# A planner that knows TensorE's array configuration and its drain, with step durations and ranks set anew

## The chip, the cores and the metric

The kernel runs on one core of a Trainium2 chip. The metric is the time of one execution on the device in microseconds, as the median of several runs; a profiled execution has its own time, given below. The core has five engines that run beside each other, each through its own list of instructions in order: TensorE (PE in the profile: matmuls and transposes), VectorE (DVE), ScalarE (ACT), GpSimd (POOL) and SyncE (SP, which issues most DMA transfers).

## What is computed

The reference, cut to what matters:

```python
# attention: q, k, v (4, 8, 576, 64), s (4, 8, 576)
scores = scale * np.matmul(q, k.transpose(0, 1, 3, 2))
cum = np.cumsum(np.maximum(s, 0.0), axis=-1)
bias = -(cum[:, :, :, None] - cum[:, :, None, :])
scores = np.where(causal, -1e9, scores + np.minimum(bias, 0.0))
x = softmax(scores) @ v                       # x: (4, 576, 512)
# gated value: a causal convolution over 5 positions gives the gate
gate = sigmoid(sum(conv_w[k] * xp[:, k:k + S, :] for k in range(5)))
x = (gate * (x @ w_val)) @ w_out
# experts: one of 8 per token, kept from the token before where a local gate says so
h = np.maximum(x[b, s] @ w1[e], 0.0)
out[b, s] = p[e] * (h @ w2[e])
```

## The kernel before, in words

The kernel has two parts. The first computes attention, the gated value, the product with `w_out` ("x2") and the routing of tokens to experts. The second (`ffn`) runs the eight experts in an order written by hand.

**Attention** goes by 16 pairs of heads (4 batches x 4 pairs). For a pair, q and k are turned on TensorE (`qk_main`, `qk_rest` for the last 64 rows), and split into a high and a low part (ScalarE, VectorE). `unit` makes the scores of a tile of 128 rows: for the tiles t < 4 both heads at once, each on 64 rows of the array (eight matmuls, line 653); for the last tile (t = 4) on the whole array (line 648). VectorE takes the minimum out of PSUM (680, 693), ScalarE the exponential (701), GpSimd scales (725), TensorE turns the result (737), ScalarE copies it out, and `pv` multiplies with v, one head in each half of the array's columns (789). Pairs 0, 1 and 4 (`LAY`) turn q and k by column halves too (533). Then GpSimd splits x (`hi`, `lo`, 803 and 807), VectorE makes the gate's five taps (814, 816) and ScalarE its tanh (821).

**value** (eight groups of twelve matmuls a batch, line 868) multiplies with `w_val`; VectorE multiplies with the gate (874). **x2_tile** (929) multiplies with `w_out`, in two halves of columns; **route** places tokens by VectorE scans and small transposes (1020, 1049). The weights `w_val` and `w_out` arrive as 64-bit numbers; `from_f64` turns them into 32-bit ones in five steps, on VectorE but for an absolute value that stands on ScalarE where `f64A` is 1 (272). `warm_up` adds steps of three small matmuls (415) that compute nothing; there are `nwarm` of them.

**The planner.** All these steps are not written out in order. Each is added to a `Plan` with its engine, an estimate of its duration, the steps it follows, the buffers (`slot`s) it holds and a rank (lower is sooner). `Plan.order` then simulates the engines: again and again it takes for each engine the first step by rank that could start at once, or else the one that can start earliest, and of these the earliest of all. The order found is the order in which the instructions are given to the engines; on the chip only that order is left of the plan, and each engine waits in it for its inputs. `SIZES` says how many buffers a name has: 4 "s" banks of PSUM for scores and pv, 2 "t" banks for the turned weights, 2 "m" banks for the turns of q and k, value, x2 and routing, 2 of "x", 5 of "xh", "xl" and "g". `RANKS` holds the numbers from which the ranks are made: for pair p the attention steps have about p, the taps p + `tap`, the split p + `split`, the value groups of batch b 4b + 4 + `val` + `dval` i, and so on. The plan doubles the duration of a TensorE step where TensorE was little used in the window before (`WINDOW`, `DUTY`).

Of the kernel before, what the change touches and what calls it, by code (L numbers as in the profile page):

```python
# [35 lines left out]
LAY = (0, 1, 4)  # L36
# [6 lines left out]
RANKS = dict(pv=-2.111, split=3.54, tap=31.589, load=2.389, front=1.118, norm=0.295, val=-0.561, dval=1.983, x2=19.035, dx2=-0.809, x2b=18.109, dx2b=2.149, x2h=16.913, send=47.523, split15=2.926, r2=11.61, xe=51.526, w=0.265, wo=1.268, nwarm=41, qP=2, merge=1, r0=10.835, r1=10.302, f64A=1, dwo=1.405)  # L43
WINDOW = 10.24 / 3
DUTY = 0.43
ISSUE = 0.6
NEXT = {"ACT": 0.06, "DVE": 0.13, "Pool": 0.1}
# [4 lines left out]
class Step:  # L52


    def __init__(self, eng, cost, f, after, on, rank, lat, rows):
        self.eng, self.cost, self.f, self.after, self.on, self.rank, self.lat = eng, cost, f, after, on, rank, lat
        self.fin, self.rows = None, rows
# [10 lines left out]
class Plan:  # L68
# [8 lines left out]
    def add(self, eng, cost, f, *after, on=(), rank=None, lat=0.17, rows=1.0):  # L77
        if eng == "PE" and lat < 1:
            lat += 0.06
        st = Step(eng, cost, f, after, on, self.rank if rank is None else rank, lat, rows)  # L80
        for sl in on:
            sl.left += 1
        self.steps.append(st)
        return st

    def order(self):
        n = len(self.steps)
        place = {st: i for i, st in enumerate(sorted(self.steps, key=lambda st: st.rank))}
        waits, users, at = {}, {st: [] for st in self.steps}, dict.fromkeys(self.steps, 0.0)
        ready = {st.eng: [] for st in self.steps}  # L90
# [4 lines left out]
        for st in self.steps:  # L95
            before, todo = set(), list(st.after)
            while todo:
                a = todo.pop()
# [10 lines left out]
        free = dict.fromkeys(ready, 0.0)  # L109
        held = {tag: [] for tag in self.sizes}  # L110
        order, use, moved = [], {}, 0.0
# [13 lines left out]
        while len(order) < n:  # L125
            best = None
            for eng, steps in ready.items():
                first = None
                for _, st in steps:
                    t = max(free[eng], at[st], opens(st))  # L130
                    if first is None or t < first[0]:
                        first = (t, st)
                        if t <= free[eng]:
                            break
                if first and (best is None or first[0] < best[0]):
                    best = first
            t, st = best
# [9 lines left out]
            if st.eng == "PE" and cost:  # L147

                if use.get(int(t / WINDOW) - 1, 0.0) < DUTY * WINDOW:
                    cost *= 2  # L150
                a, rest = t, cost
                while rest > 1e-9:
                    w = int(a / WINDOW + 1e-9)
                    d = min(rest, (w + 1) * WINDOW - a)
                    use[w] = use.get(w, 0.0) + d * st.cost / cost * st.rows
                    a, rest = a + d, rest - d
# [19 lines left out]
def build(tc, q, k, v, s, w_val, conv_w, w_out, w_gate, w_local, w1, w2, out, dbg=None):  # L176
    nc = tc.nc
    with ExitStack() as ctx:
# [23 lines left out]
        def c_pe(n):  # L202
            return n / 2350
# [75 lines left out]
        def constants():  # L279
# [33 lines left out]
            ready["ident"] = add("Pool", 1.1, lambda: make_identity(nc, ident), rank=-9)  # L313
            ready["zeros"] = add("Pool", 0.6, zeros, rank=-5)
            ready["mask"] = add("Pool", 1.6, triangles, rank=-4)
            ready["small"] = add("Pool", 1.5, small_ones, rank=0.5)
# [30 lines left out]
        def bias_rows():  # L347
# [51 lines left out]
            w = ready["gr_set"] = add("Pool", 2.6, gr_set, on=[sg])  # L399
            c = add("DVE", 1.1, scan, d, o, on=[ss, s1, sc])  # L400
            k, r = None, []
            for z in range(2):
                k = add("DVE", 0.68 if z else 0.4, lambda z=z: keys(z), c, w, k, on=[sc, sg])
                p = R["qP"] > z
                r.append(add(*(("Pool", 1.0) if p else ("ACT", 0.95)), lambda z=z, p=p: queries(z, p), k, on=[sg]))
# [114 lines left out]
        def qk_main(p, nm, loaded, sn, free):  # L520
# [27 lines left out]
            t = add("PE", 1.05 if p in LAY else 0.43, turn, loaded, ready["ident"], free, on=[sn, sm])  # L548
# [49 lines left out]
        def attention(p):  # L598
# [31 lines left out]
            def unit(u):  # L630
# [27 lines left out]
                for z in range(2 if t == 4 else 1):  # L658
                    m = add("PE", c_pe(4 * N), lambda z=z: prod(z), kq, r_, bd,
                            on=into + (banks[z:z + 1] if t == 4 else banks))  # L660
                    qk_read[p].append(m)
                    for i in (z,) if t == 4 else range(2):
                        ms[i] = m
# [161 lines left out]
            for half in range(2):  # L825
                sps = slot("s")
                m = add("PE", 2.4 if half else 0.72, lambda half=half: pv(half), evs[half], vl, rv[0],
                        on=[sps, sx, sv, rv[1]])
                pv_done[p][half] = m
                xo.append(add("ACT", c_act(320 if half else 256), lambda half=half: x_out(half), m, on=[sps, sx]))  # L830
# [18 lines left out]
        def value(b, ranks, after=None, sm_tag="m"):  # L849
# [5 lines left out]
            for i in range(8):  # L855
# [39 lines left out]
                m = add("PE", c_pe(12 * 288), prod, al, [x[0] for x in xd], [w_done[j] for j in range(4)],  # L895
# [10 lines left out]
        def x2_tile(b, t, ranks):  # L906
# [11 lines left out]
            for c0, c1, rank in ((256, WO, ranks[0]), (0, 256, ranks[1])):  # L918
# [35 lines left out]
                a = add("PE", c_pe(12 * (c1 - c0)), prod, y_steps[b, 0], y_steps[b, 1] if t > 1 else None,  # L954
# [169 lines left out]
        def route(b):  # L1124
# [5 lines left out]
            def step(eng, cost, f, *after, on=(), lat=0.17):  # L1130
                r.append(add(eng, cost, f, r[-1:], *after, on=on, lat=lat))
                return r[-1]
# [13 lines left out]
            step("DVE", 1.75, lambda: one[b].rank())  # L1146
# [521 lines left out]
```

## Time and profile before

| | us |
|---|---|
| median of 3 runs | 619.55 (618.77 to 622.70) |
| profiled execution | 616.59 |
| its span, first to last instruction | 614.8 |
| first matmul of the experts (line 1375) starts at | 363.53 |
| mean granted TensorE clock | 0.984 |

Busy times are of the hardware profiler. TensorE's matmuls are pipelined and overlap each other in the records, so their start times are what tells the pace. "Granted clock" 1.00 is 2.4 GHz, 0.50 is 1.2 GHz.

### The profile page before, as it was taken

How to read it: one execution, taken by the hardware profiler on the slowest of the kernel's cores; microseconds unless marked ns; L12 is line 12 of the kernel's file. 1: busy time of each engine (PE TensorE's matmuls, PEld its weight loads, DVE VectorE, ACT ScalarE, POOL GpSimd, SP SyncE). 2: the span in 40 equal slices, each digit the busy share in tenths (PEclk: the TensorE clock that was granted, in tenths of full speed). 3: DMA queues.
4: the chain of work that ended last, by engine and by line, in shares of the span. 5: the costliest groups of instructions: out<-in, count | busy, mean ns of one | idle time of the engine just before them, and what ended most of it. 6: DMA issues, size and time to landing. Idle time of an engine off the chain costs nothing. (4 is left out here: it accounts for less than half of the span.)

```text
span 614.8 us, 12466 instructions
## 1 busy us (share of the span) xinstructions
PE 577.8 (94%) x4346; PEld 503.3 (82%) x4346; DVE 410.5 (67%) x1029; ACT 339.4 (55%) x869; POOL 243.7 (40%) x377
## 2 busy tenths in 40 slices
PE   5899989999899988999989989999999999999994
PEld 4677678778777887777979987898998999999894
DVE  5589999968887668886699356455353636465550
ACT  2669868787478953677334325544243536355440
POOL 8367868553543433464550344030404004033101
PEclk8989999999999998999999999999999999999997
DMA  7734322322132310210133725273645537365710
GB/s 163 130 92 144 91 81 77 86 55 64 46 87 64 81 47 27 63 28 29 26 125 136 139 59 164 79 245 111 196 171 171 190 107 253 104 244 171 263 47 29
DMA packets 82838, 68.96 MB, mean 112 GB/s; under 512 B 60557, under 2 KB 66829, under 8 KB 82740
## 3 DMA queue, kind: packets, MB, share of 16 engines
q1 hardware_dynamic: 78788, 58.24, 33.2%
q0 software_dynamic: 3984, 9.88, 4.8%
q8 instruction: 36, 0.59, 0.4%
q14 instruction: 30, 0.25, 0.2%
HBM read 57.90 MB, written 10.79 MB: 112 GB/s over the span
## 5 line engine op out<-in xcount | busy, mean ns | idle before, releaser
L725 POOL TENSOR_SCALAR tt<-tt,st 128x512 f32<-128x512 f32 (+2 forms) x144 | 93.0, 661 | 103.0 <-DVE st L714 52.0
L1308 DVE TENSOR_TENSOR wl<-raw,wh 128x1024 fp32r<-128x1024 f32 x64 | 78.3, 1224 | 34.2 <-ACT wh L1305 33.8
L701 ACT ACTIVATE tt<-tt,st 128x384 f32<-128x384 f32 (+3 forms) x144 | 83.2, 583 | 12.4 <-DVE st L680 8.6
L1375 PE MATMUL h<-xth,wh 128*128 128x256 f32 (+5 forms) x256 | 73.7, 306 | 1.4 <-DVE xtl L1115 1.4
L1375 PE MATMUL h<-xth,wl 128*128 128x256 f32 (+5 forms) x256 | 72.9, 302 | 0.0
L680 DVE CUSTOM_DVE_ANT_0 tt<-s,mask 128x512 f32<-128x512 f32 (+3 forms) x128 | 57.9, 483 | 13.9 <-PE s L653 7.5
L1458 POOL DMA_INDIRECT out_dram<-out,id x21 | 28.6, 1362 | 96.7 <-ACT out L1456 83.3
L1305 ACT ACTIVATE wh<-raw 128x1024 fp32r<-128x1024 f32 x64 | 66.5, 1052 | 0.3 <-DMA raw<-in_moe_w_dram 0.3
L816 DVE SCALAR_TENSOR_TENSOR g<-x,cw,g 128x576 f32<-128x576 f32 x64 | 64.8, 1012 | 0.7
L737 PE MATMUL t<-ident,tt 128*128 128x128 f32 x384 | 61.9, 283 | 3.5 <-POOL tt L725 2.2
L1381 ACT ACTIVATE hh<-h 128x256 fp32r<-128x256 f32 (+5 forms) x64 | 27.1, 425 | 58.5 <-PE h L1375 52.1
L1382 DVE SCALAR_TENSOR_TENSOR hl<-h,hh 128x256 fp32r<-128x256 f32 (+5 forms) x64 | 29.8, 469 | 43.4 <-ACT hh L1381 43.4
L737 PEld LDWEIGHTS t<-ident,tt 128*128 128x128 f32 x384 | 43.3, 142 | 15.7 <-POOL tt L725 8.1
L1340 POOL DMA_INDIRECT xg<-x2d,id x20 | 20.9, 1046 | 87.2 <-DMA id<-ids 59.2
L929 PE MATMUL x<-wo_h,yl 128*128 128x266 f32 (+3 forms) x144 | 43.2, 300 | 7.8 <-DVE y L874 2.9
L653 PE MATMUL s<-QK 64*128 64x256 f32 (+2 forms) x384 | 48.9, 356 | 1.2 <-DVE st L693 1.2
L1375 PEld LDWEIGHTS h<-xth,wh 128*128 128x128 f32 x256 | 48.3, 189 | 1.9 <-DVE xtl L1115 1.6
L1375 PEld LDWEIGHTS h<-xth,wl 128*128 128x128 f32 x256 | 48.4, 189 | 0.2
L789 PE MATMUL pv<-PT,nv 128*64 128x320 f32 (+3 forms) x384 | 47.3, 386 | 0.0
L1375 PE MATMUL h<-xtl,wh 128*128 128x256 f32 (+5 forms) x256 | 46.3, 302 | 0.0
L929 PE MATMUL x<-wo_h,yh 128*128 128x266 f32 (+3 forms) x144 | 41.6, 289 | 0.0
L929 PE MATMUL x<-wo_l,yh 128*128 128x266 f32 (+3 forms) x144 | 41.6, 289 | 0.0
(269 smaller groups left out, 1499.4 us busy)
## 6 DMA issues: line engine op xcount, KB each, us to landing
raw<-in_moe_w_dram SPq DMA_DIRECT2D x64, 512.0 KB
nv<-in_v_dram SPq DMA_DIRECT2D x32, 128.0 KB
x2d<-x SPq DMA_DIRECT2D x32, 128.0 KB
nk<-in_k_dram SPq DMA_DIRECT2D x26, 128.0 KB
nq<-in_q_dram SPq DMA_DIRECT2D x26, 128.0 KB
wsc<-in_moe_w_val_dram SPq DMA_DIRECT2D x4, 512.0 KB
wsc<-in_moe_w_out_dram SPq DMA_DIRECT2D x4, 512.0 KB
nk<-in_k_dram SPq DMA_DIRECT2D x3, 256.0 KB
```

The lines of the kernel that those rows point to most:

```text
L653: nc.tensor.matmul(ps[hh][:, 0:N], lhsT=q[:, P * t:P * t + P], rhs=k[:, 0:N], start=n == 0, stop=n == 3)
L680: nc.vector.tensor_tensor_reduce(out=tl["tt"][:, 0:W], in0=ps[h][:, 0:W], in1=mask[:, 512 - W:512], scale=1.0, scalar=3.0e38, op0=ALU.add, ...
L701: nc.scalar.activation(tt[:, 0:W], tt[:, 0:W], AF.Exp, bias=st[:, 0, i:i + 1], scale=-1.0, accum_out=st[:, 1, i:i + 1])
L725: nc.gpsimd.tensor_scalar(tl["tt"][:, 0:W], tl["tt"][:, 0:W], st_["st"][:, 2, i:i + 1], 1.0, ALU.mult, ALU.mult)
L737: nc.tensor.transpose(ps[:, j], tl["tt"][:, P * j:P * j + P], ident)
L789: nc.tensor.matmul(tl["ps", half][64 * h:64 * h + 64, c:c + w], lhsT=vt[0:K, j, h] if j < 4 else vr[:, 2 * hp + h], rhs=(PT1 if half else ...
L816: nc.vector.scalar_tensor_tensor(tl["g"], x[:, t:t + S], cw[:, hp, t:t + 1], tl["g"], ALU.mult, ALU.add)
L929: nc.tensor.matmul(ps[0:m, 0:c1 - c0], lhsT=yy[:, kc] if both else yy[:, kc, P * t:P * t + m], rhs=wt_[:, kc, c0:c1], start=n == 0, stop=n ...
L1305: nc.scalar.activation(hi, raw, AF.Copy)
L1308: nc.vector.tensor_tensor(lo, raw, fv(hi), ALU.subtract)
L1375: nc.tensor.matmul(ps[:, 0:N], lhsT=w[:, P * f:P * f + P], rhs=xx[:, kc, c], start=n == 0, stop=n == 11)
L1382: nc.vector.scalar_tensor_tensor(hl[:, c], ps[:, 0:N], 0.0, fv(hh[:, c]), ALU.max, ALU.subtract)
```

## The change

The planner's model of TensorE is changed and all numbers that it works with are set anew. What each engine computes stays the same, but for three choices in `RANKS`: no warm-up steps (`nwarm` 41 to 0), one of the two query rows of the bias on ScalarE instead of GpSimd (`qP` 2 to 1), and the absolute value in the conversion of weights on VectorE instead of ScalarE (`f64A` 1 to 0).

A step gets a `mode`: "whole" (the default), "rows" (scores of t < 4) or "columns" (pv, and the turns of q and k of the pairs in `LAY`). In `order`, when the first TensorE step by rank has another mode than the last one, a step of the same mode that can start within 0.05 us and whose rank is at most `R_MODE` (2.332) higher is taken instead. A change of mode costs `SWITCH` (0.2 us) in the plan. The durations of matmul groups get a part for each matmul, and several durations of other engines are changed. The diff, cut to its core:

```diff
@@ -40,10 +40,12 @@
     return ap.bitcast(F32)
-RANKS = dict(pv=-2.111, split=3.54, tap=31.589, load=2.389, front=1.118, norm=0.295, val=-0.561, dval=1.983, x2=19.035, dx2=-0.809, x2b=18.109, dx2b=2.149, x2h=16.913, send=47.523, split15=2.926, r2=11.61, xe=51.526, w=0.265, wo=1.268, nwarm=41, qP=2, merge=1, r0=10.835, r1=10.302, f64A=1, dwo=1.405)
+RANKS = dict(pv=-14.891, split=3.794, tap=15.492, load=2.105, front=1.145, norm=0.197, val=-11.824, dval=0.089, x2=25.546, dx2=-5.125, x2b=11.419, dx2b=3.236, x2h=37.933, send=63.151, split15=1.095, r2=-13.208, xe=68.451, w=20.124, wo=-0.731, nwarm=0, qP=1, merge=1, r0=-2.243, r1=-0.613, f64A=0, dwo=1.274)
 WINDOW = 10.24 / 3
 DUTY = 0.43
 ISSUE = 0.6
+SWITCH = 0.2
+R_MODE = 2.332
 NEXT = {"ACT": 0.06, "DVE": 0.13, "Pool": 0.1}
 SIZES = dict(m=2, s=4, t=2, n=4, qk=2, G=2, gr=1, st=3, tt0=2, tt1=3, tt2=3, tt3=3, tt4=2, x=2, g=5, xh=5, xl=5, y=2,
              raw=4, x2=4, w=1, wf=1, nq=1, nk=1, nv=1, rq=1, rk=1, rv=1, lgs=4)
@@ -52,9 +54,9 @@
 class Step:
-    def __init__(self, eng, cost, f, after, on, rank, lat, rows):
+    def __init__(self, eng, cost, f, after, on, rank, lat, rows, mode):
         self.eng, self.cost, self.f, self.after, self.on, self.rank, self.lat = eng, cost, f, after, on, rank, lat
-        self.fin, self.rows = None, rows
+        self.fin, self.rows, self.mode = None, rows, mode
 class Slot:
@@ -74,10 +76,10 @@
     def slot(self, tag):
         return Slot(tag)
-    def add(self, eng, cost, f, *after, on=(), rank=None, lat=0.17, rows=1.0):
+    def add(self, eng, cost, f, *after, on=(), rank=None, lat=0.12, rows=1.0, mode="whole"):
         if eng == "PE" and lat < 1:
-            lat += 0.06
-        st = Step(eng, cost, f, after, on, self.rank if rank is None else rank, lat, rows)
+            lat += 0.18
+        st = Step(eng, cost, f, after, on, self.rank if rank is None else rank, lat, rows, mode)
         for sl in on:
             sl.left += 1
         self.steps.append(st)
@@ -108,7 +110,7 @@
                 arrive(st)
         free = dict.fromkeys(ready, 0.0)
         held = {tag: [] for tag in self.sizes}
-        order, use, moved = [], {}, 0.0
+        order, use, moved, mode = [], {}, 0.0, "whole"
         def opens(st):
@@ -125,13 +127,17 @@
         while len(order) < n:
             best = None
             for eng, steps in ready.items():
-                first = None
+                first = other = None
                 for _, st in steps:
                     t = max(free[eng], at[st], opens(st))
                     if first is None or t < first[0]:
                         first = (t, st)
-                        if t <= free[eng]:
-                            break
+                    if eng == "PE" and st.cost and st.mode == mode and other is None and t <= free[eng] + 0.05:
+                        other = (t, st)
+                    if t <= free[eng] and (eng != "PE" or other or st.rank > first[1].rank + R_MODE):
+                        break
+                if other and first[1].mode != mode and other[1].rank <= first[1].rank + R_MODE:
+                    first = other
                 if first and (best is None or first[0] < best[0]):
                     best = first
             t, st = best
@@ -145,6 +151,9 @@
                     held[sl.tag].append(sl)
             cost = st.cost
             if st.eng == "PE" and cost:
+                if st.mode != mode:
+                    mode = st.mode
+                    t = max(t, free["PE"] + SWITCH)
                 if use.get(int(t / WINDOW) - 1, 0.0) < DUTY * WINDOW:
                     cost *= 2
@@ -199,8 +208,8 @@
         TURN = (0, 256, 512)
-        def c_pe(n):
-            return n / 2350
+        def c_pe(n, k=1):
+            return k * (n / 2400 + 0.0133)
         def c_act(n):
             return 0.05 + n / 1200
@@ -310,10 +319,10 @@
                 nc.gpsimd.memset(floor[0:1], float(EARLY))
             ready["zb"] = add("DVE", 0.1, lambda: nc.vector.memset(zb, 0.0), rank=-9)
-            ready["ident"] = add("Pool", 1.1, lambda: make_identity(nc, ident), rank=-9)
-            ready["zeros"] = add("Pool", 0.6, zeros, rank=-5)
-            ready["mask"] = add("Pool", 1.6, triangles, rank=-4)
-            ready["small"] = add("Pool", 1.5, small_ones, rank=0.5)
+            ready["ident"] = add("Pool", 0.6, lambda: make_identity(nc, ident), rank=-9)
+            ready["zeros"] = add("Pool", 3.1, zeros, rank=-5)
+            ready["mask"] = add("Pool", 2.6, triangles, rank=-4)
+            ready["small"] = add("Pool", 2.4, small_ones, rank=0.5)
             sb, sz = slot("xh"), slot("xl")
@@ -396,13 +405,13 @@
                 out=tl["s"][32 * h:32 * h + 16], in_=s.rearrange("b (p two) s -> two (b p) s", two=2)[h]), a, on=[ss],
                 lat=FAR) for h in range(2)]
             o = add("DVE", 0.6, one_set, on=[s1])
-            w = ready["gr_set"] = add("Pool", 2.6, gr_set, on=[sg])
-            c = add("DVE", 1.1, scan, d, o, on=[ss, s1, sc])
+            w = ready["gr_set"] = add("Pool", 3.0, gr_set, on=[sg])
+            c = add("DVE", 1.76, scan, d, o, on=[ss, s1, sc])
             k, r = None, []
             for z in range(2):
                 k = add("DVE", 0.68 if z else 0.4, lambda z=z: keys(z), c, w, k, on=[sc, sg])
                 p = R["qP"] > z
-                r.append(add(*(("Pool", 1.0) if p else ("ACT", 0.95)), lambda z=z, p=p: queries(z, p), k, on=[sg]))
+                r.append(add(*(("Pool", 1.7) if p else ("ACT", 0.95)), lambda z=z, p=p: queries(z, p), k, on=[sg]))
             ready["gr"], ready["gr_slot"] = (tl, r), sg
             ready["gates"] = [add("SP", 0.91, lambda h=h: nc.sync.dma_start(
                 out=gates[:, h].rearrange("p r k s -> p (r k) s"),
@@ -545,7 +554,8 @@
             def lo():
                 src, h_, l_ = views()
                 nc.vector.scalar_tensor_tensor(l_, src, sc, fv(h_), ALU.mult, ALU.subtract)
-            t = add("PE", 1.05 if p in LAY else 0.43, turn, loaded, ready["ident"], free, on=[sn, sm])
+            t = add("PE", 1.05 if p in LAY else 0.43, turn, loaded, ready["ident"], free, on=[sn, sm],
+                    mode="columns" if p in LAY else "whole")
             a = add("ACT", 0.5, hi, t, on=[sm])
             z = add("DVE", 0.62, lo, a, on=[sm])
             return a, z
@@ -656,7 +666,7 @@
                 keep = [slot(f"tt{t}") for _ in mine]
                 into = keep + [place(u)[2][0]]
                 for z in range(2 if t == 4 else 1):
-                    m = add("PE", c_pe(4 * N), lambda z=z: prod(z), kq, r_, bd,
+                    m = add("PE", c_pe(N, 4) + (t < 4) * 0.1, lambda z=z: prod(z), kq, r_, bd, mode="whole" if t == 4 else "rows",
                             on=into + (banks[z:z + 1] if t == 4 else banks))
                     qk_read[p].append(m)
                     for i in (z,) if t == 4 else range(2):
@@ -824,8 +834,8 @@
             xo = []
             for half in range(2):
                 sps = slot("s")
-                m = add("PE", 2.4 if half else 0.72, lambda half=half: pv(half), evs[half], vl, rv[0],
-                        on=[sps, sx, sv, rv[1]])
+                m = add("PE", 2.35 if half else 0.8, lambda half=half: pv(half), evs[half], vl, rv[0],
+                        mode="columns", on=[sps, sx, sv, rv[1]])
                 pv_done[p][half] = m
                 xo.append(add("ACT", c_act(320 if half else 256), lambda half=half: x_out(half), m, on=[sps, sx]))
             attn.extend(plan.steps[n0:])
@@ -892,7 +902,7 @@
                         nc.vector.scalar_tensor_tensor(l_, y, 0.5, fv(h_), ALU.mult, ALU.subtract)
                 xd = [xs_done[b * NP + kc] for kc in range(4)]
                 gd, sg = g_done[b * NP + oc]
-                m = add("PE", c_pe(12 * 288), prod, al, [x[0] for x in xd], [w_done[j] for j in range(4)],
+                m = add("PE", c_pe(288, 12), prod, al, [x[0] for x in xd], [w_done[j] for j in range(4)],
                         on=[sm] + [sl for x in xd for sl in x[1]])
                 e = add("DVE", c_dve(288) + 0.05, ev, m, gd, on=[sm, sy, sg])
                 more = b in MERGE and z == 1
@@ -951,7 +961,7 @@
                     if end:
                         tc.declare_no_dep(i.ins, group="early rows", reason="the last batch's rows are out of bounds there")
                         tc.add_to_no_dep_group("last rows", i.ins)
-                a = add("PE", c_pe(12 * (c1 - c0)), prod, y_steps[b, 0], y_steps[b, 1] if t > 1 else None,
+                a = add("PE", c_pe(c1 - c0, 12), prod, y_steps[b, 0], y_steps[b, 1] if t > 1 else None,
                         y_steps[0, 1] if both else None, [w_done[j] for j in range(4, 8)],
                         on=[sm, yr["slot"]] if both else [sm])
                 if not both:
@@ -1143,7 +1153,7 @@
                 a = add("PE", 0.45 if c < 512 else 0.22, lambda c=c: one[b].turn(c), start, on=[sm])
                 a = add("ACT", 0.26 if c < 512 else 0.1, lambda c=c: one[b].keep(c), a, on=[sm])
                 step("DVE", 0.35, lambda c=c: one[b].fill(c), a, on=[sm])
-            step("DVE", 1.75, lambda: one[b].rank())
+            step("DVE", 2.24, lambda: one[b].rank())
             sm = slot(tag)
             step("PE", 0.25, lambda: one[b].back(), on=[sm])
             placed = step("DVE", 0.12, lambda: one[b].place(), on=[sm])

```

## Rows read from the trace of the kernel before

**Rows 1.** The page: the span, and each engine's busy time, share and instructions.

```profile
span 614.8 us, 12466 instructions
PE 577.8 (94%) x4346; PEld 503.3 (82%) x4346; DVE 410.5 (67%) x1029; ACT 339.4 (55%) x869; POOL 243.7 (40%) x377
```

**Rows 2.** Busy us (xinstructions) by stretch: PE, PEld, DVE, ACT, POOL; granted clock, DMA share, GB/s.

```profile
0.00:363.50 363.50, 336.85 (x2799) 277.87 (x2799) 286.24 (x841) 230.18 (x694) 187.40 (x305) 0.98 0.33 82
363.50:614.80 251.30, 240.95 (x1547) 225.39 (x1547) 124.30 (x188) 109.27 (x175) 56.30 (x73) 0.99 0.46 156
...
0.00:20.00 20.00, 12.86 (x114) 10.36 (x116) 12.01 (x33) 5.78 (x13) 16.53 (x59) 0.83 0.65 136
...
40.00:120.00 80.00, 75.62 (x657) 58.44 (x656) 77.26 (x223) 63.20 (x196) 58.68 (x72) 1.00 0.37 98
```

**Rows 3.** Waits of PE, 0 to 364 us: total us, times, longest.

```profile
PE qk L561 <- DVE QK L547: 3.4, 2, 2.8
PE x L929 <- DVE y L874: 2.9, 1, 2.9
PE x L929 <- DVE lgs L941: 2.6, 1, 2.6
PE x L929 <- ACT x L935: 2.3, 1, 2.3
```

**Rows 4.** Timeline (start us, us, what) of DVE and POOL around the 2.6 us wait.

```profile
158.72 3.29 POOL L807 TENSOR_TENSOR xl<-x,xh 128x576 fp32r<-128x576 f32 x2
158.75 2.01 DVE L816 SCALAR_TENSOR_TENSOR g<-x,cw,g 128x576 f32<-128x576 f32 x1
```

**Rows 5.** Timeline of PE from 253.0 to 254.1 us.

```profile
253.04 0.27 PE L737 MATMUL t<-ident,tt 128*128 128x128 f32 x1
253.15 0.27 PE L739 MATMUL t<-ident,tt 128*64 128x128 f32 x1
253.35 0.63 PE L653 MATMUL s<-QK 64*128 64x256 f32 x6
253.81 0.28 PE L653 MATMUL s<-G 64*128 64x256 f32 x2
254.02 0.33 PE L737 MATMUL t<-ident,tt 128*128 128x128 f32 x1
```

**Rows 6.** Groups of PE, 0 to 363.5 us: busy us, mean ns, idle before.

```profile
L653 PE MATMUL s<-QK 64*128 64x256 f32 (+2 forms) x384 | 48.9, 356 | 1.2 <-DVE st L693 1.2
```

**Rows 7.** Busy us of value (line 868) on PE and PEld in one stretch.

```profile
319.40:336.80 17.40, 13.52 (x96) 12.87 (x96) 1.00 0.45 148
```

**Rows 8.** Busy us of the warm-up matmuls (line 415) by stretch.

```profile
20.00:40.00 20.00, 3.10 (x36) 2.19 (x36) 0.91 0.67 136
40.00:120.00 80.00, 1.91 (x21) 1.54 (x21) 1.00 0.37 98
```

**Rows 9.** Timeline of the first 20 us, cut.

```profile
4.00 1.16 PE L533 MATMUL kT<-ident,nk 128*64 128x128 f32 x16
...
10.41 0.27 PE L561 MATMUL qk<-ident,rq 64*128 64x64 f32 x1 [2.79 <-DVE QK L547]
...
12.96 1.64 POOL L390 TENSOR_SCALAR gr<-gr 48x512 fp32r<-48x512 f32 x3
...
13.21 1.98 PE L533 MATMUL kT<-ident,nk 128*64 128x128 f32 x16
...
15.26 1.13 POOL L390 TENSOR_SCALAR gr<-gr 48x512 fp32r<-48x512 f32 x3
...
16.10 1.45 SPq L590 DMA_DIRECT2D G<-gr  x2
```

**Rows 10.** Groups by line, 0 to 364 us: the absolute value, and the taps.

```profile
L816 DVE SCALAR_TENSOR_TENSOR g<-x,cw,g 128x576 f32<-128x576 f32 x64 | 64.8, 1012 | 0.7
...
L814 DVE TENSOR_SCALAR g<-x,cw 128x576 f32<-128x576 f32 x16 | 13.1, 817 | 9.1 <-ACT x L799 9.1
...
L272 ACT ACTIVATE wsc<-wsc 128x512 f32<-128x512 f32 x8 | 5.4, 681 | 3.3 <-DVE wf_in_moe_w_val_dram L267 3.0 <-ACT tt L701 0.3
```

## The prediction

> **What bounds the kernel now.** I read the busy times of the page first, then the busy times by stretch, then the waits of TensorE, then the timeline where those waits lie. The page [rows 1] shows TensorE busy for 94% of a span of 614.8 us, no other engine over 67%. By stretch [rows 2] the kernel has two halves. In 0 to 363.5 us the planner's order runs (attention, value, x2, routing); from 363.5 us to the end the experts run, whose order is written by hand and which the diff does not touch. So only the first 363.5 us can move. There TensorE is busy 336.85 us: 26.65 us are idle. 7.14 us of these lie in the first 20 us, where data arrive; the other 19.5 us lie behind. From 40 to 120 us VectorE is nearly full too, 77.26 of 80 us, beside TensorE's 75.62: in that stretch both set the pace, afterwards TensorE does.
>
> The waits of TensorE [rows 3] say who ends the idle time. The longest are few: 3.4 us at the start for the first q and k, then 2.9, 2.6 and 2.3 us of x2 steps that wait for VectorE or ScalarE, two of them for a bank to be emptied. The timeline around the 2.6 us [rows 4] shows why VectorE was late: while GpSimd runs two splits of x (3.29 us for two), a tap takes 2.01 us, where the mean of all 64 taps is 1.01 us [rows 10]. The 2.9 us lie behind the same pair.
>
> **The change, part by part.** The sum is made against the profiled execution, 616.59 us with a span of 614.8; the median of the three runs, 619.55, is 2.96 us above it, so each saving is taken from either.
>
> A. Changes of array configuration. In [rows 5] all runs at granted clock 1.00 (2.4 GHz). Two transposes of one configuration start 0.11 us apart (253.04, 253.15); the first score matmul, on 64 rows, starts 0.20 us after the last transpose: 0.09 us for going in. Going out: six score matmuls, three pairs, take 0.46 us from 253.35 to 253.81, so 0.15 for a pair; the last pair (253.81) is followed by a whole-array matmul 0.21 us later: 0.06 us. A way in and out thus costs 0.15 us; I use 0.08 for one change. Counted along the timeline of TensorE between the first (warm-up to kT at 4.00) and the last (routing at 358.8) there are 182 changes, 91 excursions, about 15 us. How many can the new choice save? The first part has 64 score steps of eight matmuls, six of them on q and k (384 records, [rows 6]), 16 turns of the last 64 rows (32 records in pairs), 32 pv halves and 6 two-column turns of q and k: 118 steps in another configuration, of which 27 already stand behind one of their own kind. If all score steps and all pv halves went in pairs there would be 32 + 16 + 16 + 6 = 70 excursions, 21 fewer, 3.4 us. More is excluded: a score step fills two of four "s" banks, so a third in a row has to wait for VectorE, and the choice takes only steps that can start within 0.05 us. The turn of the last 64 rows keeps the default "whole", so the planner does not see its two changes. Bounds 0 to -3.4; I take -2.5, nearer to the full pairing because the choice may reach 2.332 ranks ahead.
> The Trainium skill, page "TensorEngine Tiling (Array Packing)", section Restrictions and Gotchas, says that row tiles raise the demand for PSUM, different row tiles writing to different banks. The code agrees (each head of a score step has its own bank); no row here shows the banks apart. Were it to forbid pairs altogether, term A would be 0 and the sum -6.5 instead of -9.
>
> B. No warm-up matmuls (41 to 0 steps). Of their 123 records 57 run between 20 and 120 us [rows 8]; the others lie ahead of the data or in the gaps of the routing chain. The 57 cover 1.91 us in 40 to 120 us and 3.10 in 20 to 40: at most 5.0 us to gain, if each had delayed real work. Against it stands the clock. kT's sixteen matmuls take 1.16 us at 4.00 (granted clock high after the warm-up) and 1.98 at 13.21 (low clock, 1.2 GHz): without warm-up the first two turns lose 0.8 us each, 1.6 in all. The 2.79 us wait at 10.41 for VectorE [rows 9] hides that; with this cover gone it is +1.6. I take -0.5.
>
> C. One of the two query rows moves from GpSimd to ScalarE. GpSimd does them at 12.96 (1.64 us) and 15.26 (1.13 us), and the bias rows go out behind the second, at 16.10 [rows 9]. With the second on ScalarE beside the first they could go out when the first ends, at 14.60 instead of 16.39: at most -1.8; nothing, if scores are still placed behind the turns of pair 1. I take -1. The corrected costs of GpSimd's set-up (zeros 3.1 where 0.6 stood) move nothing by themselves, since GpSimd takes these in the order of rank, as before.
>
> D. The absolute value of the weight conversion moves to VectorE: 8 instructions of 0.68 us leave ScalarE [rows 10]; taken at the same length on VectorE that is about 5.5 us more there. Where VectorE is full (40 to 120 us) each costs its whole length; later it hides behind TensorE. The new ranks put four conversions (w_out) early, at -0.7 to 3.1, and four (w_val) at 20 and more, where they fill gaps: four early ones are 2.7 us. Bounds 0 to +5.5; I take +2.
>
> E. Order and durations. The old plan gave a value group 1.47 us (12 x 288 / 2350); eight take 13.52 us [rows 7], 1.69 each; the new one gives 1.60. Over 32 value groups that is some 7 us by which the plan believed TensorE early, and the unpriced changes of A are another 15 us, so the other engines were ordered for a TensorE 22 us faster than it is. A truer plan should put what frees banks earlier. What it can win is the idle time behind the first 20 us, 19.5 us, without the 7.8 us of the three x2 waits [rows 3]: neither plan has a cost for VectorE being stretched by GpSimd [rows 4]. Of the 11.7 left I take 60%: -7. Bounds: -19.5, and above zero, since every rank is new and a wait can as well be made longer.
>
> Sum: -2.5 - 0.5 - 1 + 2 - 7 = -9.0, so 607.6 in a profiled execution and 610.5 as a median.
>
> **The rivals.**
> 1. Nothing moves. Banks and ready times allow hardly a pair (A = 0) and the new order trades old waits for new ones (E = 0): -0.5 - 1 + 2 = +0.5, 620. For it: the largest waits have a cause outside the plan. Against it: mis-sized steps of 7 and 15 us are a real fault of the old plan.
> 2. VectorE and the "m" banks become the bound: slower. Value steps now have rank 4b - 7.8, before all else (they were spread from 3.4 to 17.3 for the first batch), while the taps they need stand at p + 15.5. A value group holds one of two "m" banks until VectorE has multiplied with the gate, and the turns of the next pair's q and k use the same two banks. One pair's taps cost 0.82 + 4 x 1.01 = 4.9 us [rows 10]. If one pair's taps are open when the groups of two batches start: +9.8; D in full instead of in part: +3.5; E lost: +7. From -9 that gives +11.3, 631. It decides as soon as value groups wait more than some 2 us for a gate. For it: 77 of 80 us of VectorE in 40 to 120. Against: the taps' rank is lower than before (31.6), so earlier, and the planner sees both banks.
> 3. Much more is won: pairs everywhere (-3.4) and all 19.5 us of idle time: -3.4 - 0.5 - 1 + 2 - 19.5 = -22.4, 597. For it: TensorE's 26.65 us of idle time are mostly short waits that a good order could cover. Against: 7.8 of it is GpSimd's doing.
>
> **How the numbers follow.** About 1% (6.2 us) is what a measurement of this kernel can tell from no change: under 613.4 is faster, over 625.7 slower. The forecast (603 to 616, its own range) gets 0.43, of which 0.35 lies under 613.4; rival 1 (614 to 626) 0.27, all but 0.02 within 1%; rival 2 (622 to 640) 0.18, of which 0.15 is slower; rival 3 0.12, all faster. Faster 0.35 + 0.12 = 0.47; same 0.08 + 0.25 + 0.03 = 0.36; slower 0.17. The range leaves out about 0.05 of rival 3 below 598 and 0.12 of rival 2 above 627.
>
> **What the profile after would show.** A: in the PE timeline, score steps in pairs, and under 150 changes. B: no L415 rows, granted clock of 0 to 20 us below 0.83. C: bias rows issued before 16 us. D: no ScalarE row for the absolute value and VectorE's busy time in the first part some 5 us up. E: TensorE's idle time behind 20 us near 12 us; the first expert matmul at about 354 us instead of 363.5. Expert part unchanged at 251 us. Wrong would be: waits of value groups or of q and k turns for taps or banks (rival 2), or as much idle time as before under other names (rival 1).

## The result

The changed kernel takes 624.27 us (median of 19 runs) beside 620.53 for the kernel before: the ratio is 1.0058, with a 95% interval of 1.0037 to 1.0079. That is 3.6 us slower: inside the 1% that the prediction called no change, but the interval leaves out 1, and 9 us faster was forecast.

The page of the changed kernel, then its busy us by stretch (columns as in [rows 2]: PE, PEld, DVE, ACT, POOL, granted clock, DMA share, GB/s):

```profile
span 622.5 us, 12227 instructions
PE 573.2 (92%) x4223; PEld 500.3 (80%) x4223; DVE 412.9 (66%) x1038; ACT 334.6 (54%) x863; POOL 250.2 (40%) x374
```

```profile
0.00:371.20 371.20, 332.30 (x2676) 274.94 (x2677) 287.99 (x848) 225.27 (x688) 190.71 (x299) 0.98 0.32 80
371.20:622.50 251.30, 240.93 (x1547) 225.38 (x1547) 124.89 (x191) 109.32 (x175) 59.45 (x75) 0.99 0.49 156
0.00:20.00 20.00, 11.51 (x90) 9.52 (x91) 12.33 (x35) 6.36 (x15) 15.71 (x56) 1.00 0.83 149
20.00:371.20 351.20, 320.79 (x2588) 265.42 (x2587) 275.66 (x814) 218.91 (x674) 175.00 (x243) 0.98 0.29 76
40.00:120.00 80.00, 69.86 (x579) 50.87 (x575) 75.99 (x217) 58.34 (x185) 56.11 (x70) 0.98 0.35 87
```

Beside [rows 2]: the experts take 251.3 us as before, the whole difference of 7.7 us between the two profiled spans lies in the first part. The profiled execution of the kernel before (616.59 us) lies 3.9 us under its median here (620.53), so about half of the 7.7 us belongs to that one execution. In the first part TensorE is busy 4.5 us less (332.30 for 336.85; 123 warm-up matmuls and 33 changes of configuration are gone), but idle 38.9 us instead of 26.65; behind the first 20 us it is idle 30.4 us, where the kernel before shows 19.5 and the prediction named 12. From 40 to 120 us it is busy 69.86 instead of 75.62. Who ended its waits in the first part (total us, times, longest):

```profile
PE t L747 <- POOL tt L735: 5.2, 5, 1.4
PE t L747 <- ACT PT L760: 4.1, 5, 1.9
PE t L747 <- ACT PT L762: 3.8, 3, 1.8
PE kT L542 <- DMA nk<-in_k_dram: 3.6, 1, 3.6
...
PE x L939 <- DVE y L884: 1.3, 1, 1.3
...
PE x L939 <- DVE lgs L951: 0.3, 1, 0.3
```

The long x2 waits of [rows 3] have shrunk. In their place stand 15 waits, of about 1 us in the mean, of the turns ("t", line 747; 737 before) for GpSimd to scale a tile or for ScalarE to empty a bank: 13.8 us in all, where those of the kernel before come to 3.5:

```profile
PE t L737 <- POOL tt L725: 2.2, 4, 0.8
...
PE t L737 <- ACT PT L750: 1.1, 2, 0.8
...
PE t L737 <- ACT PT L747: 0.2, 1, 0.2
```

One of them, in the changed kernel's timeline of PE, of DVE, and of POOL and ACT, from 64 us:

```profile
64.41 0.88 PE L747 MATMUL t<-ident,tt 128*128 128x128 f32 x6
...
65.12 0.96 PE L483 MATMUL wp<-wg,woT 128*128 128x10 f32 x8
...
67.87 0.57 PE L747 MATMUL t<-ident,tt 128*128 128x128 f32 x3 [1.79 <-ACT PT L762]
```

```profile
64.00 1.75 DVE L826 SCALAR_TENSOR_TENSOR g<-x,cw,g 128x576 f32<-128x576 f32 x1
65.68 0.68 DVE L690 CUSTOM_DVE_ANT_0 tt<-s,mask 128x512 f32<-128x512 f32 x1
```

```profile
64.05 1.09 POOL L464 TENSOR_TENSOR wo_l<-wf_in_moe_w_out_dram,wo_h 128x512 fp32r<-128x512 f32 x1
...
65.10 1.92 POOL L817 TENSOR_TENSOR xl<-x,xh 128x576 fp32r<-128x576 f32 x1
...
66.46 0.72 ACT L711 ACTIVATE tt<-tt,st 128x512 f32<-128x512 f32 x1 [1.48 <-DVE st L690]
...
67.34 0.38 ACT L762 ACTIVATE PT<-t 128x256 f32<-128x256 f32 x1
```

A tap (L826) takes 1.75 us while GpSimd runs two-input subtractions from 64.05 to 67.02: first the low part of `w_out` (L464), then that of x (L817). The minimum (L690) behind the tap is late, ScalarE waits 1.48 us for it, empties the bank late (L762), and TensorE's turn, next in its list, waits 1.79 us.

### The profile page after: what moved, and what is told of

It reads as the page before. It is cut to its first block, busy times and chain, and to the rows that moved or that the text cites. A ratio compares the mean times of both kernels' runs of the same rounds, so it can differ in the third digit from the quotient of the medians.

```text
span 622.5 us, 12227 instructions
## 1 busy us (share of the span) xinstructions
PE 573.2 (92%) x4223; PEld 500.3 (80%) x4223; DVE 412.9 (66%) x1038; ACT 334.6 (54%) x863; POOL 250.2 (40%) x374
## 5 line engine op out<-in xcount | busy, mean ns | idle before, releaser
L735 POOL TENSOR_SCALAR tt<-tt,st 128x512 f32<-128x512 f32 (+2 forms) x144 | 96.6, 685 | 90.7 <-DVE st L724 37.6
L711 ACT ACTIVATE tt<-tt,st 128x384 f32<-128x384 f32 (+4 forms) x144 | 83.3, 582 | 32.4 <-DVE st L690 22.6
L747 PE MATMUL t<-ident,tt 128*128 128x128 f32 x384 | 61.7, 285 | 15.3 <-POOL tt L735 5.2
L690 DVE CUSTOM_DVE_ANT_0 tt<-s,mask 128x512 f32<-128x512 f32 (+3 forms) x128 | 56.8, 483 | 11.2 <-PE s L663 9.5
L826 DVE SCALAR_TENSOR_TENSOR g<-x,cw,g 128x576 f32<-128x576 f32 x64 | 61.7, 963 | 0.5
L1350 POOL DMA_INDIRECT xg<-x2d,id x20 | 22.6, 1132 | 84.1 <-DMA id<-ids 32.2
L799 PE MATMUL pv<-PT,nv 128*64 128x320 f32 (+3 forms) x384 | 49.0, 395 | 0.1
L939 PE MATMUL x<-wo_h,yl 128*128 128x256 f32 (+3 forms) x144 | 43.7, 304 | 4.1 <-DVE y L884 1.3
L939 PE MATMUL x<-wo_l,yh 128*128 128x256 f32 (+3 forms) x144 | 41.6, 289 | 0.0
L939 PE MATMUL x<-wo_h,yh 128*128 128x256 f32 (+3 forms) x144 | 41.5, 288 | 0.0
```

The source lines that it names most:

```text
L690: nc.vector.tensor_tensor_reduce(out=tl["tt"][:, 0:W], in0=ps[h][:, 0:W], in1=mask[:, 512 - W:512], scale=1.0, scalar=3.0e38, op0=ALU.add, ...
L711: nc.scalar.activation(tt[:, 0:W], tt[:, 0:W], AF.Exp, bias=st[:, 0, i:i + 1], scale=-1.0, accum_out=st[:, 1, i:i + 1])
L735: nc.gpsimd.tensor_scalar(tl["tt"][:, 0:W], tl["tt"][:, 0:W], st_["st"][:, 2, i:i + 1], 1.0, ALU.mult, ALU.mult)
L747: nc.tensor.transpose(ps[:, j], tl["tt"][:, P * j:P * j + P], ident)
L799: nc.tensor.matmul(tl["ps", half][64 * h:64 * h + 64, c:c + w], lhsT=vt[0:K, j, h] if j < 4 else vr[:, 2 * hp + h], rhs=(PT1 if half else ...
L826: nc.vector.scalar_tensor_tensor(tl["g"], x[:, t:t + S], cw[:, hp, t:t + 1], tl["g"], ALU.mult, ALU.add)
```

## The experiments

All ratios are to the kernel before on the same chip, with 95% intervals; what is said against the changed kernel is the difference to its 1.0058. Three theories came first: **clock** (the warm-ups are missed), **order** (the new ranks order badly), **planner** (grouping and durations order badly). After the first runs a fourth was added, **fit**: ranks serve only the planner with which they were found.

### Warm-ups

The old order without the matmuls of the warm-ups (b_nowarm):

```diff
-                    warm(ps_m.tile([P, 512], F32, tag="m", name=f"warm_{i}"), 3)
+                    ps_m.tile([P, 512], F32, tag="m", name=f"warm_{i}")
```

> The kernel before in its own, unchanged order; the 41 warm-up steps stand in the plan as before, but issue no matmul. Theory 'clock' (the changed kernel lost because without warm-ups more of TensorE's real work runs at the low clock, and the warm-ups only filled idle time): slower than before by 4 to 6 us, ratio 1.006 to 1.010, with more low-clock stretches behind 20 us and as much idle time more as the warm-ups took (10 us). Theory 'order' (warm-ups cost and gave nothing; the loss sits in the new order): ratio 0.998 to 1.002.

Measured: 0.9969 (0.9942 to 0.9996), 1.9 us faster. "Clock" falls. Its busy us from 0 to 367:

```profile
0.00:367.00 367.00, 334.01 (x2677) 275.29 (x2677) 285.51 (x841) 229.75 (x694) 188.88 (x305) 0.98 0.33 81
```

TensorE is idle 33.0 us, 6.3 more than in [rows 2]: the warm-ups had mostly filled idle time, as expected. More low-clock stretches did come (the granted clock of 20 to 40 us is 0.83 instead of 0.91), but the warm-ups cost more than they saved. This kernel is the fair comparison for the changed one, which has no warm-ups either. Its idle time by stretch and its waits of turns:

```profile
0.00:20.00 20.00, 9.24 (x74) 7.48 (x74) 10.94 (x30) 5.68 (x13) 18.09 (x59) 1.00 0.65 127
20.00:367.00 347.00, 324.77 (x2603) 267.81 (x2603) 274.57 (x811) 224.07 (x681) 170.78 (x247) 0.98 0.31 78
```

```profile
PE t L737 <- POOL tt L725: 2.9, 5, 0.8
...
PE t L737 <- ACT PT L747: 1.8, 4, 0.6
...
PE t L737 <- ACT PT L750: 0.8, 1, 0.8
```

The changed kernel is idle 5.9 us more (38.9 against 33.0): 8.2 us more behind the first 20 us (30.4 against 22.2) and 2.3 us less ahead of that. Its turns wait 13.8 us against 5.5.

The changed kernel with warm-ups, `nwarm=0` to `nwarm=41`, planned anew:

> The changed kernel with nwarm 41 again, planned anew. Theory 'clock': 4 to 6 us faster than the changed kernel, ratio to before 0.996 to 1.000, low-clock stretches behind 20 us back to two. Theory 'order': within 2 us of the changed kernel, ratio 1.003 to 1.009; if the warm-ups are in the way of real work, slower than it.

Measured: 1.0199 (1.0141 to 1.0258), 8.7 us slower than the changed kernel. Giving it warm-ups does not help it; what they cost can't be told here from what the new order costs.

### Planner and ranks apart

Old `RANKS` in the changed kernel:

> The changed planner (configuration, drain, new durations) with all of the old RANKS. Theory 'order' (the new ranks, w_val's late conversion first of all, take the work away that fills 40 to 120 us): ratio 0.990 to 0.997, the saved changes of configuration (some 33 x 0.08 us) stay as a gain. Theory 'clock': about 0.996 to 1.000, since the warm-ups are back. Theory 'planner' (grouping and the new durations themselves order worse for the chip): 1.006 or more.

New `RANKS` in the kernel before:

> The old planner with all of the new RANKS. Theory 'order': as slow as the changed kernel or slower by the 2.6 us of configuration changes it doesn't save, ratio 1.006 to 1.012. Theory 'clock': the same, 1.006 to 1.012, as it has no warm-ups either; the low-clock stretches tell. Theory 'planner': faster than the changed kernel, 0.995 to 1.002.

Measured: 1.0318 (1.0254 to 1.0381) and 1.0213 (1.0155 to 1.0271). Either half of the change alone is two to three per cent slower; only together are they near the old time. So neither "order" nor "planner" is the whole story. (`RANKS` holds `nwarm`, `qP` and `f64A` too, so these go back and forth with the ranks.) The halves of the planner, with old ranks: durations alone (`SWITCH = 0.0`, `R_MODE = -1e9`), and configuration alone (old durations):

> The kernel before with the new durations alone: old RANKS, a change of configuration costs nothing (SWITCH 0) and nothing is grouped. Theory 'durations' (the new durations make the planner order worse for the chip): ratio 1.02 to 1.035. Theory 'grouping' (keeping to a configuration puts off what other engines wait for): 0.995 to 1.005. Theory 'fit' (ranks serve only the planner that they were found with, whichever part of it is altered): 1.01 to 1.03.

> The kernel before with configuration, drain and grouping alone: old RANKS, old durations. Theory 'grouping': ratio 1.02 to 1.035, about as a_oldranks. Theory 'durations': 0.992 to 1.000, the saved drains as a gain. Theory 'fit': 1.01 to 1.03.

Measured: 1.0156 (1.0132 to 1.0180) and 1.0267 (1.0231 to 1.0304). Both cost, as "fit" says. With the new ranks, grouping off:

```diff
-R_MODE = 2.332
+R_MODE = -1e9
```

> The changed kernel with grouping off (R_MODE -1e9), the drain still in the plan, new RANKS. Theory 'grouping': faster than the changed kernel, ratio to before 0.990 to 1.000, TensorE's waits for turns (15 us) back to some 5. Theory 'fit': slower than the changed kernel, 1.012 to 1.03, and over 170 changes of configuration.

Measured: 1.0102 (1.0081 to 1.0124), 178 changes of configuration: 0.4% slower than the changed kernel, between the two expectations. The waits of the turns fall only to 10 us: most of them are there without grouping. Two trifles in the old planner test "fit" without any truer or falser model, `lat=0.17` to `lat=0.16` and ScalarE's `0.05` to `0.06`:

> The kernel before with one number of the plan changed by a trifle: the wait between engines 0.16 us instead of 0.17. It says nothing truer or falser of the chip; only the order changes. Theory 'fit' (the old ranks are one lucky order among many, and any change of the planner leaves it): ratio 1.008 to 1.025. Theory 'worse model' (the new durations and the grouping order worse because of what they are): 0.996 to 1.004.

> The kernel before with another trifle: ScalarE's fixed part 0.06 us instead of 0.05. Theory 'fit': ratio 1.008 to 1.025. Theory 'worse model': 0.996 to 1.004.

Measured: 1.0043 (1.0017 to 1.0068) and 1.0072 (1.0037 to 1.0107). Smaller than "fit" said, but both are slower. A change of the plan that means nothing costs 0.4 to 0.7%: as much as the whole change did, and as much as switching the grouping off, whose 0.4% can therefore not be put down to the grouping itself.

### Single causes

The absolute value back on ScalarE, in the changed kernel's own order (a_absact):

```diff
-                if R["f64A"]:
+                if True:
                     nc.scalar.activation(fv(hi), fv(hi), AF.Abs)
```

> The changed kernel in its own, unchanged order, with the eight absolute values issued on ScalarE at the places where the plan has them on VectorE. If VectorE's 5.5 us more are part of the loss (term D): 2 to 5 us faster than the changed kernel, ratio to before 0.998 to 1.003. If they hide: within 1.5 us of it, 1.003 to 1.008.

Measured: 1.0026 (0.9999 to 1.0053), 2.0 us faster than the changed kernel, and the two intervals together leave about 2 us either way: it agrees with term D, without confirming its size.

`w_val` converted early again, `w=20.124` to `w=0.265`:

> The changed kernel with w_val's conversions early again (w 0.265 instead of 20.124), planned anew. Theory 'late w_val' (value starts at 138 us instead of 90, and till then TensorE has only attention and waits for its turns): 3 to 6 us faster than the changed kernel, ratio to before 0.996 to 1.001, first value near 105 us, waits of turns under 8 us. Theory 'fit' (one number of a tuned set put back leaves the order that was found): slower than the changed kernel, 1.010 to 1.022.

Measured: 1.0083 (1.0056 to 1.0110). Value starts at 107 us instead of 138 and turns wait 8 us instead of 15, but the turns of q and k wait 12 us instead of 9, and TensorE starts the experts at the same time, 371 us. "Late w_val" falls: the wait moved. The time lies in neither expected range.

GpSimd's subtraction of x left out, in the new order (a_lozero) and in the old one (b_lozero); the low part of x is zero there:

```diff
-                nc.gpsimd.tensor_tensor(tl["xl"], tl["x"][:, 4:580], fv(tl["xh"]), ALU.subtract)
+                nc.gpsimd.memset(fv(tl["xl"]), 0.0)
```

> The changed kernel in its own order; the low part of x is left out (GpSimd writes zeros in place of the subtraction that reads two tiles), so that GpSimd no longer stretches VectorE there. Theory 'GpSimd beside VectorE' (the plan's missing cost makes the waits of turns and x2): 4 to 10 us faster than the changed kernel, ratio to before 0.990 to 0.999, taps all near 0.82 us. Otherwise: within 2 us of it.

> The same in the kernel before: the low part of x left out, the order unchanged. Theory 'GpSimd beside VectorE': the two x2 waits of 2.6 and 2.9 us vanish, 5 to 8 us faster than before, ratio 0.987 to 0.992. If the changed kernel gains more by it than this one, the new order meets the stretched VectorE more often; if as much, its loss lies elsewhere.

Measured: 0.9900 (0.9868 to 0.9931) and 0.9779 (0.9734 to 0.9825): 10 us less than the changed kernel and 14 us less than the kernel before, where 5 to 8 were expected. This step costs both kernels more than the change moved, but the old order gains more by its absence, so it does not explain why the new order is slower. Of the changed kernel's turn waits (14.8 us, with those for the split of x and for VectorE) 13.3 us stay, the wait of 1.79 us shown above among them (1.78 here). The tap ahead of that one still takes 1.75 us, since the low part of `w_out` is still subtracted on GpSimd beside it; no run left out these subtractions of the weights. In the kernel before the x2 waits fall from 7.8 to 1.9 us, as the prediction's reading of [rows 4] had it; the waits at the top of its list are now these:

```profile
PE qk L561 <- DVE QK L547: 3.4, 2, 2.8
PE s L653 <- DMA G<-gates: 2.2, 1, 2.2
PE qT L529 <- issue: 1.6, 1, 1.6
PE t L737 <- POOL tt L725: 1.5, 3, 0.7
```

### Ranks searched further, and a faster kernel

Ranks for the new planner searched further against the planner's own end, the time at which its simulation finishes:

> The changed kernel with RANKS searched further against its own planner, whose own end falls by about 3.4 us. If the new planner's forecast of differences holds on the chip (and the change lost because its ranks stopped short): 2 to 5 us faster than the changed kernel, ratio to before 0.997 to 1.003. If such small differences do not carry over: anything from 1.000 to 1.012.

Measured: 1.0027 (0.9997 to 1.0058), some 2 us faster than the changed kernel by the ratios, but the two intervals overlap, and both expected ranges hold 1.0027. The run does not tell whether a forecast of 3.4 us carries over; it brought no order that beats the one before.

VectorE computes the low part, in the old order (b_lodve_fixed) and planned anew (b_lodve):

```diff
-                nc.gpsimd.tensor_tensor(tl["xl"], tl["x"][:, 4:580], fv(tl["xh"]), ALU.subtract)
+                nc.vector.tensor_tensor(tl["xl"], tl["x"][:, 4:580], fv(tl["xh"]), ALU.subtract)
```

> The kernel before in its own order, the low part of x computed by VectorE at the place where GpSimd did it. Theory 'GpSimd beside VectorE': VectorE gets 16 x some 0.7 us = 11 us more, and loses about as much stretching of taps; the x2 waits go: ratio 0.982 to 0.994. If VectorE now waits for the high part that GpSimd has still to write: 0.997 to 1.01.

> The same, planned anew with the low part as a VectorE step of 0.68 us, old planner and old RANKS. Theory 'GpSimd beside VectorE': 0.985 to 0.998; the new order may cost 0.4 to 0.7 per cent as the two trifles did.

Measured: 0.9905 (0.9878 to 0.9931) in the old order, faster than both kernels, and 0.9981 (0.9951 to 1.0011) planned anew: again some 0.8% for a new order. The groups of the first, VectorE's taps and its new step:

```profile
L816 DVE SCALAR_TENSOR_TENSOR g<-x,cw,g 128x576 f32<-128x576 f32 x64 | 55.3, 864 | 0.6
...
L807 DVE TENSOR_TENSOR xl<-x,xh 128x576 fp32r<-128x576 f32 x16 | 13.0, 813 | 0.0
```

VectorE takes 13.0 us on and gives 9.5 us of stretched taps back (64.8 in [rows 10]). Its split of y (L892) gives back 3.7 us more (15.6 us here, 19.3 in the kernel before), so the step costs VectorE next to nothing, and GpSimd is rid of it. Last, both planners with this step on VectorE and ranks searched for the same time:

> The changed planner, the low part of x on VectorE (0.68 us in the plan), RANKS searched against the planner's own end for the same time as in b_lodve_search. If the new planner orders better once the cost it lacks is gone and both are searched alike: faster than b_lodve_search, ratio to before 0.975 to 0.987. If it doesn't: 0.985 to 0.998 and not faster than b_lodve_search.

> The old planner, the low part of x on VectorE, RANKS searched against the planner's own end for the same time. Its own end falls by some 12 us against b_lodve with old RANKS. If the old planner's forecast of differences holds: ratio to before 0.975 to 0.988; if what it leaves out (drains, each matmul's own part) misleads it: 0.99 to 1.01.

Measured: 0.9949 (0.9923 to 0.9974) for the new planner, 0.9798 (0.9753 to 0.9843) for the old, 605.08 us. The old planner's forecast of some 12 us against b_lodve holds (0.9981 to 0.9798 is 11.3). The kernel that it ordered, with wrong durations and no notion of configurations, is faster by 1.5%, at more changes (163 against 149). Both searches dropped the warm-ups and chose `qP=1`; the old planner's kept `f64A=1`, the new one's `f64A=0`, which by a_absact can be about 2 us of the 9.3. It is one search each. Their first parts from 0 to the first expert matmul, new planner first:

```profile
0.00:362.90 362.90, 330.46 (x2676) 274.27 (x2676) 290.35 (x866) 225.99 (x688) 170.28 (x288) 0.98 0.34 82
```

```profile
0.00:352.90 352.90, 328.01 (x2676) 273.65 (x2677) 287.54 (x857) 231.95 (x697) 163.17 (x284) 0.98 0.35 84
```

Idle time makes most of the 10 us between these two: 32.4 against 24.9 us.

## Why the prediction was wrong

**A held in count.** Counted as in the prediction there are 149 changes of configuration for 182, 33 fewer; at 0.08 us that is 2.6 us, 2.5 were forecast. Five of the 33 went with the warm-ups (177 changes in b_nowarm), which leaves 2.2 us for the ordering. Its time was not measured alone: grouping off costs 0.4%, but so does a trifle.

**B was right in sign.** -0.5 was taken, -1.9 measured (b_nowarm, in the old order). The slow start came as costed: kT and qT at the low clock, with VectorE's next wait behind them.

```profile
3.65 1.98 PE L542 MATMUL kT<-ident,nk 128*64 128x128 f32 x16 [3.65 <-DMA nk<-in_k_dram]
7.26 1.97 PE L542 MATMUL qT<-ident,nq 128*64 128x128 f32 x16 [1.63 <-DMA nq<-in_q_dram]
11.04 0.36 PE L571 MATMUL qk<-ident,rq 64*128 64x64 f32 x1 [1.81 <-DVE QK L556]
```

The wait for VectorE shrank from 2.79 us [rows 9] to 1.81, as cover. Only the sign named for it in the profile was wrong: the granted clock of 0 to 20 us reads 1.00, although 1.98 us for sixteen matmuls is what [rows 9] show at the low clock; the first clock record of this trace stands at 18.05 us, and the column reads 1.00 ahead of it.

**C came, by another way than reasoned.** The bias rows go out 2.2 us earlier (16.10 in [rows 9]):

```profile
13.10 1.04 ACT L401 ACTIVATE gr<-gr 48x512 fp32r<-48x512 f32 x3
...
13.92 1.51 SPq L600 DMA_DIRECT2D G<-gr  x2
```

ScalarE's row runs behind GpSimd's and not beside it; 1.5 us of the 2.2 come from GpSimd's row, which starts at 11.45 instead of 12.96. What it is worth shows against b_nowarm, the old order without warm-ups, where the first matmuls that read the bias wait for it; in the changed kernel they don't wait. b_nowarm first:

```profile
20.08 1.44 PE L653 MATMUL s<-G 64*128 64x512 f32 x2 [2.31 <-DMA G<-gr]
```

```profile
18.27 0.39 PE L663 MATMUL s<-G 64*128 64x512 f32 x2
```

They start 1.8 us earlier, where -1 was taken. How much of it reaches the end was not tested alone.

**D's net agrees, its parts were off**: +2 forecast, 2.0 measured, give or take 2 (a_absact). The prediction priced the eight instructions on VectorE at ScalarE's 0.68 us; there they take 0.50, 4.0 us and not 5.5:

```profile
L283 DVE TENSOR_SCALAR wsc<-wsc 128x512 int32<-128x512 int32 x8 | 4.0, 499 | 0.0
```

The four of `w_val` do not fill late gaps as reasoned: three of them run between 72 and 120 us, where VectorE is full. VectorE's busy time in the first part rises by 1.8 us (287.99 for 286.24), not by the 5 named as a sign, since its taps are stretched less here (61.7 us for 64.8) and its split of y too (16.5 for 19.3). That +2 came out is partly luck.

**E failed**, and with it the whole. It reasoned that a plan with truer durations puts the work in a better order and took -7 us. From the measured +3.6 the others (A -2.2, B -1.9, C 0 to -1.8, D +2.0) leave +5.7 to +7.5 us for it; by the intervals of the measured terms that is an estimate good to about 3 us either way. The idle time agrees: behind 20 us the changed kernel has 8.2 us more than b_nowarm, with D's 2 among them, where E was to take 7 off. The fault was to read E off the plan's errors: the old order came from the old ranks and the old, wrong durations together, and that pair was good; the new pair, with truer durations, is no better. The four pairs of planner and ranks (1, 1.0213, 1.0318, 1.0058) show that the two can't be judged apart, and two trifles (1.0043, 1.0072) that even a meaningless disturbance leaves the good order. Of the eleven orders planned anew with GpSimd's step in place, the changed kernel's among them, none was faster than the old one. "Bounds above zero" was written and then given no weight in a sum; rival 1 (E = 0, 620, range 614 to 626) is nearest, and its reason, that the largest waits have a cause outside the plan, was right of the x2 waits (b_lozero).

**Rival 2** is not what happened: value groups wait 0.7 us in all, and no wait of the turns of q and k is ended by a tap or a value group.

**What stays open** is why the new planner's order is the worse one even when its ranks are searched as long (0.9949 against 0.9798, with `f64A` and the luck of one search each in it), and how the old order came to be so good: how its ranks were found, and whether it was picked by its time on the chip, is not on record. One reading would be that the old plan, in which TensorE is too fast, has its inputs ready by the time the real TensorE comes, while the truer one takes turns at the moment their inputs should be there, and any lateness of GpSimd or ScalarE becomes a wait; the waits of turns (13.8 us against 5.5 in b_nowarm) fit it. That is only argued; no run slowed the other engines in the plan to try it.

## What to carry to other kernels

A planner's order and the ranks tuned for it are one thing: here a corrected model with the old ranks cost 1.6 to 3.2%, and the truer model did not win after a new search either. Before a new order is given credit or blame, time a meaningless change of the plan; here it costs 0.4 to 0.7%. Look first for costs that no version of the plan has: one GpSimd step beside VectorE was worth 1% by being moved, in the old order, and 2% with ranks searched for it (0.3% of these by dropping the warm-ups, if b_nowarm carries over).

## What the runs showed of the hardware

Two-input GpSimd steps hold VectorE up: 25.6 us of subtractions in the kernel before cost it 14 us end to end (b_lozero, with GpSimd's 16 us saved among them), and taps go from a mean of 1012 ns to 861 without them. The Trainium skill, page "SBUF — State Buffer", section "SBUF: two separate sides", says why: VectorE steps with two inputs in SBUF and GpSimd steps that read it share one pair of ports under an exclusive lock, and the later one waits out the whole instruction. The traces agree. In [rows 4] the tap starts just behind this subtraction and ends at 160.76, 0.62 us after it:

```profile
158.72 1.42 POOL L807 TENSOR_TENSOR xl<-x,xh 128x576 fp32r<-128x576 f32 x1
```

All nine taps that begin during a subtraction of x in the kernel before end 0.61 or 0.62 us after it, and the tap of 1.75 us above ends 0.61 us after the 1.09 us of L464. Where the tap is first, it keeps its 0.82 us and the subtraction takes 2.02 instead of 1.42:

```profile
319.73 0.82 DVE L816 SCALAR_TENSOR_TENSOR g<-x,cw,g 128x576 f32<-128x576 f32 x1
```

```profile
319.81 2.02 POOL L807 TENSOR_TENSOR xl<-x,xh 128x576 fp32r<-128x576 f32 x1
```

GpSimd's write-only fill of the same tile (0.6 us) leaves the tap beside it at 0.80, in the kernel before with the subtraction left out:

```profile
159.47 1.09 POOL L807 MEMSET xl<- 128x576 f32 x2
```

```profile
159.53 0.80 DVE L816 SCALAR_TENSOR_TENSOR g<-x,cw,g 128x576 f32<-128x576 f32 x1
```
